# A gated linear attention and its feed-forward on one Trainium2 core: one recorded list of named steps, extended from the first tokens to the second group of feed-forward

## The chip, the core and the metric

The kernel runs on one core of a Trainium2 chip. The core has five engines that run their own queues of instructions in order: PE (matrix multiply), DVE (vector), ACT (scalar functions), POOL (GpSimd) and SP, which here only issues DMAs. The metric is device time in microseconds of one launch, from runs without a profiler. Three runs of the kernel before took 487.58 to 489.64 us, with a median of 488.57 us.

## The reference, cut to what matters

```python
for t in range(S):                                    # B=4, H=8, S=768, D=40
    m_new = maximum(f[t] + m, i[t])                   # running maximum of the gates
    C = exp(f[t] + m - m_new) * C + exp(i[t] - m_new) * outer(v[t], k[t])
    n = exp(f[t] + m - m_new) * n + exp(i[t] - m_new) * k[t]
    y[t] = sigmoid(o[t]) * (C @ q[t]) / maximum(abs(n @ q[t]), 1)
x = y as (B*S = 3072 tokens, H*D = 320)
h = x @ w_in                                          # 320 -> 2048
out = (maximum(h, 0) + alpha * minimum(h, 0)) @ w_out # 2048 -> 320
```

The weights `w_in`, `w_out` arrive as 64-bit floats, the rest as 32-bit ones. Results must have nearly full 32-bit accuracy.

## The kernel before, in words

**Tiles.** The sequence is cut into chunks of 128 tokens: six for each of the four batch rows, 24 in all. Within a chunk the recurrence is written as a masked product of scores, decays and values plus a term from the state left by the chunks before. Two chunks make a group of 256 tokens for the feed-forward, so there are 12 groups.

**Feed-forward.** A group has eight up steps and eight down steps. One up step (`FeedForward.up`) makes 256 hidden channels with 16 matmuls of 256 columns each, since activations and weights are kept as a high and a low part (`XH`, `XL`, `WH`, `WL`; the last 64 of the 320 input channels are in `X2`, `X2L`, `W2`). ACT then takes the negative part (`L722`), DVE applies alpha (`L726`), ACT rounds to the high part `gh` (`L734`), and the low part `gl` is the difference (`L735`), on DVE for the first two groups and on POOL for all later ones. A down step (`L743`) is 12 matmuls of 320 columns.

**Weights.** A block of 64-bit weights is loaded as pairs of 32-bit words and turned into 32-bit floats: ACT scales the upper word (`Weights.scale`, `L816`), DVE shifts it left by three (`L828`) and joins the top bits of the lower word (`L830`). ACT then makes the high part (`L838`) and DVE the low part (`L842`). There are 8 blocks `wi`, 2 blocks `wr` and 8 blocks `wo`. They are staged in tiles that later hold `w_out` parts (`ROOM`), so a block's load waits until the room is free.

**Order.** The first group (chunks 0 and 1, the gates and part of the weights) follows `ORDER`, a string of short step names, and `pin` keeps each engine to that order. Steps named `warmN` are N matmuls of no use on the identity (`L139`); there are 107 of them. Everything after that is emitted by loops, which interleave the up and down steps of groups 0 and 1 with the attention of chunks 2 to 6 (`Side`, `attention`, `stage_a`, `stage_b`). There the compiler's scheduler sets the order in which each engine takes its instructions, and the weights of a block are turned when the loop comes to it (`convert`). From the third group on `ffn` and `late_chunk` do the same for the rest of the program.

**Masks and decays.** For chunks 0 to 3 the decays of a row are spread over the partitions by matmuls into `pb` (`L1016`, `L495`). ACT takes the exponential (`L1027`, `L501`), and POOL zeroes what lies after the token with an affine select (`L1031`, `L505`). Later chunks read the decays from DRAM (`Lb`).

Three DMA queues are in use, and nearly all loads are issued by SP in program order. One instruction there that waits for a buffer holds back all loads behind it.

Of the kernel before, what the change touches and what calls it, by code (L numbers as in the profile page):

```python
# [17 lines left out]
def kernel(ctx: ExitStack, tc: tile.TileContext, q, k, v, i_gate, f_gate, o_gate, w_in, w_out, alpha, out):  # L18
# [68 lines left out]
    pick = const.tile([3 * BH, BH], BF16, tag="pick", name="pick")  # L87

# [175 lines left out]
    def padded_tiles():  # L264


        for j in range(2):
            K = sb.tile([P, 2, 512], F32, tag="kS", name=f"kf{j}", bufs=2)
            nc.gpsimd.memset(K[64:R, 0], 0.0)
            nc.gpsimd.memset(K[:64, 1], 0.0)  # L270
            kpads.append(K)
# [7 lines left out]

    def stage_a(n):  # L280

        pq = psa(f"pq{n}")
        transposed(pq, qn_t[n % NQ])
        K = padded(n)
        qf = sb.tile([P, 512], F32, tag="qf", name=f"qf{n}")
        nc.scalar.copy(qf[:R], pq[:R])
        yield
        pk = psa(f"pk{n}")
        transposed(pk, kn_t[n % NQ])
        padded_copy(K, pk)  # L290
        chunk[n] = (None, K, qf)
        yield
        after(n)
        yield
# [189 lines left out]
    def stage_b(n):  # L484
# [4 lines left out]
        for par in range(2):  # L489
            E = sb.tile([P, 512], F32, tag="E", name=f"E{n}_{par}", bufs=4)  # L490
            if Lb is None:
                pb = psa(f"pb{n}_{par}")
                for p in range(NPR):
# [3 lines left out]
                        LP[:, n % GC * P : (n % GC + 1) * P], start=True, stop=True,  # L497
                    )
            for p in range(NPR):
# [5 lines left out]
            nc.gpsimd.affine_select(  # L505
                out=E, in_=E, pattern=[[0, NPR], [1, P]], base=0, channel_multiplier=-1,
                compare_op=ALU.is_ge, fill=0.0,
            )
# [106 lines left out]
    def attention(n0):  # L615

        late, x_due = iter(()), []
        for _ in stage_a(n0):
            yield
        for n in range(n0, B * NC):  # L620
# [3 lines left out]
            a = stage_a(n + 1) if n + 1 < NDIR else iter(())  # L624
# [24 lines left out]
            if n + 1 == NDIR:  # L649
                far = first_stacks()  # L650
                order = a, bb, late, a, bb, far, bb, far, a, far, far
# [27 lines left out]
    EARLY = 1  # L679
    S1, S2 = 4, 1  # L680
# [4 lines left out]
    V0, V1 = 0, 2  # L685
    FILL = {3: 4, 4: 14, 5: 4}
    ORDER = """dq0 dq1 dw0 dw2 warm24 dv0 dw1 dw4 do1 dw3 do2 scan lf0a lf0b li0 lf0z L0 bj0 qT0 qc0 kT0 kc0 warm12 sp00
        bTt bTc l3a l3b alT l3c l3d warm6 wt0 ex00 sc00 l3e ms00 warm3 sp01 ewj ex01 ms01 sc01 warm3 eeL wg00 wTt eTt
        wTc eTc lf1a lf1b warm3 w0s wg01 sp10 alC ex10 ms10 warm3 sp11 ex11 qT1 w1s kT1 kc1 w0j0 warm4 li1 wd0 w0j1 w2s
# [106 lines left out]
    class Weights:  # L796
# [51 lines left out]
        def all(self):  # L848
            self.scale()
            self.join()  # L850
            for piece in range(len(self.pieces)):
                self.split(piece)
# [473 lines left out]
```

## Time and profile before

| what | value |
| --- | --- |
| runs without profiler, median of 3 | 488.57 us (487.58 to 489.64) |
| profiled execution, own time | 491.87 us |
| its span, first to last instruction | 489.1 us |
| granted TensorE clock, mean | 0.997 |
| busy PE, PE weight load, DVE, ACT, POOL | 473.7, 459.0, 325.3, 310.5, 305.0 us |
| share of the DMA engines taken by packets | 56.6% of the span |
| moved by DMA | 61.60 MB, 126 GB/s over the span |

The profiled execution's own time is 2.8 us above its span, which is launch and end. A busy time counts a matmul until its modelled end, so back-to-back matmuls overlap, and how much useful work PE did is better counted by the distance from one start to the next. A line such as `L735` names the kernel's source line above. "pS<-qf,kf" names the tile that is written and those that are read, without their buffer numbers. In the view by slices a digit is the busy share of one fortieth of the span, 12.2 us.

### The profile page before, as it was taken

The page shows a single profiled execution, that of the slowest core. Times are in us where ns is not written, and L with a number is a line of the kernel's source. Part 1 is how long each engine was busy: PE and PEld are TensorE (multiplying, and loading weights), DVE is VectorE, ACT ScalarE, POOL GpSimd, SP SyncE. Part 2 cuts the span into 40 slices and gives each one's busy share as a digit, 9 for nine tenths or more (in the row PEclk, how much of TensorE's full clock was granted, in tenths as well). Part 3 has the DMA queues.
Part 4 walks back from the last instruction along what each step waited for, and adds up shares of the span by engine and source line. Part 5 has one row for each costly group of instructions (what it writes and reads, how often), then busy time and mean ns, then how long its engine had stood idle before and what let it go on. Part 6 is the DMA issues. An engine that isn't in the chain of part 4 may idle for free.

```text
span 489.1 us, 11907 instructions
## 1 busy us (share of the span) xinstructions
PE 473.7 (97%) x4509; PEld 459.0 (94%) x4509; DVE 325.3 (66%) x679; ACT 310.5 (63%) x692; POOL 305.0 (62%) x394
## 2 busy tenths in 40 slices
PE   8998889999999999999999999999989999999997
PEld 7887778899999999999989999999989999999996
DVE  7889899955676477576495584675694685774321
ACT  3769498645677567676596594776685685553332
POOL 6642063505559859967679779959489598243342
PEclk9999998999999999999999999999999999999999
DMA  9999977354595455687955376677746233000000
GB/s 176 233 167 245 247 196 209 97 107 97 136 205 114 112 138 101 146 188 125 181 146 128 66 188 96 146 168 161 138 127 130 45 99 93 28 1 2 27 1 27
DMA packets 173922, 61.60 MB, mean 126 GB/s; under 512 B 140154, under 2 KB 166122, under 8 KB 173866
## 3 DMA queue, kind: packets, MB, share of 16 engines
q1 hardware_dynamic: 173786, 60.75, 56.6%
q8 instruction: 35, 0.57, 0.5%
q14 instruction: 21, 0.17, 0.1%
q10 hardware_dynamic: 80, 0.11, 0.1%
HBM read 36.90 MB, written 4.03 MB: 84 GB/s over the span
## 4 chain that ended last, share of the span: by engine, by line
PE 66%; DVE 9%; DMA 8%; POOL 6%; issue 4%; ACT 4%; SPq 1%; ACTq 0%; DVEq 0%; POOLq 0%
PE po L743 26%; PE ph L713 4%; PE ph L720 4%; PE ph L717 3%; PE ph L719 3%; PE ph L716 3%; PE ph L714 3%; PE ph L715 3%; PE ph L718 3%; DMA wo<-in_moe_w_out_dram 3%; PE pH L349 3%; DMA qS<-Z 3%; PE pS L445 2%; PE warm L139 2%; POOL gl L735 2%
## 5 line engine op out<-in xcount | busy, mean ns | idle before, releaser
L735 POOL TENSOR_TENSOR gl<-g,gh 128x512 fp32r<-128x512 f32 x80 | 103.0, 1289 | 61.8 <-ACT gh L734 49.3
L726 DVE SCALAR_TENSOR_TENSOR g<-g,oma,ph 128x256 f32<-128x256 f32 x160 | 69.6, 476 | 87.4 <-ACT g L722 82.7
L743 PE MATMUL po<-OH,gh 128*128 128x320 f32 x368 | 109.9, 311 | 0.8 <-ACT gh L734 0.6
L743 PE MATMUL po<-OL,gh 128*128 128x320 f32 x368 | 109.7, 311 | 0.0
L722 ACT ACTIVATE g<-ph 128x512 f32<-128x512 f32 x96 | 57.1, 596 | 44.1 <-PE ph L720 36.2
L734 ACT CAST gh<-g 128x512 fp32r<-128x512 f32 x80 | 49.6, 620 | 41.1 <-DVE g L726 39.8
L743 PEld LDWEIGHTS po<-OH,gh 128*128 128x128 f32 x368 | 69.2, 188 | 1.4 <-ACT gh L734 1.4
L743 PE MATMUL po<-OH,gl 128*128 128x320 f32 x368 | 70.3, 312 | 0.0
L743 PEld LDWEIGHTS po<-OL,gh 128*128 128x128 f32 x368 | 68.9, 188 | 0.0
L713 PE MATMUL ph<-XH,WH 128*128 128x256 f32 x192 | 55.3, 288 | 2.1 <-DVE g L726 1.3
L743 PEld LDWEIGHTS po<-OH,gl 128*128 128x128 f32 x368 | 56.7, 188 | 0.2
L720 PE MATMUL ph<-X2L,W 128*128 128x256 f32 x192 | 54.4, 284 | 0.0
L717 PE MATMUL ph<-X,W 128*128 128x256 f32 x192 | 54.1, 283 | 0.0
L716 PE MATMUL ph<-XH,WL 128*128 128x256 f32 x192 | 54.1, 282 | 0.0
L719 PE MATMUL ph<-XL,WH 128*128 128x256 f32 x192 | 54.1, 282 | 0.0
L714 PE MATMUL ph<-XH,WH 128*128 128x256 f32 x192 | 53.9, 281 | 0.0
L715 PE MATMUL ph<-XH,WL 128*128 128x256 f32 x192 | 53.9, 281 | 0.0
L718 PE MATMUL ph<-XL,WH 128*128 128x256 f32 x192 | 53.7, 280 | 0.0
L336 ACT CAST E<-pS 128x512 bf16<-128x512 f32 x72 | 41.5, 585 | 9.9 <-DVE pS L334 7.3
L420 ACT ACTIVATE E<-Lb,bT 128x128 f32<-128x128 f32 x136 | 42.2, 390 | 2.1 <-PE pH L349 2.0
L713 PEld LDWEIGHTS ph<-XH,WH 128*128 128x128 f32 x192 | 36.4, 190 | 3.2 <-DVE gl L735 1.1
L717 PEld LDWEIGHTS ph<-X,W 128*128 128x128 f32 x192 | 36.2, 189 | 0.0
(202 smaller groups left out, 1134.2 us busy)
## 6 DMA issues: line engine op xcount, KB each, us to landing
Lb<-L_d SPq DMA_DIRECT2D x20, 512.0 KB
wo<-in_moe_w_out_dram SPq DMA_DIRECT2D x8, 640.0 KB
wi<-in_moe_w_in_dram SPq DMA_DIRECT2D x8, 512.0 KB
qn<-in_q_dram SPq DMA_DIRECT2D x24, 160.0 KB
kn<-in_k_dram SPq DMA_DIRECT2D x24, 160.0 KB
va<-in_v_dram SPq DMA_DIRECT2D x24, 160.0 KB
og<-in_o_gate_dram SPq DMA_DIRECT2D x24, 160.0 KB
out_dram<-ob SPq DMA_DIRECT2D x11, 320.0 KB
```

The source lines that it names most:

```text
L713: nc.tensor.matmul(dst, WH[half][:, 0, hs], XH[:, 0], start=True, stop=False)
L714: nc.tensor.matmul(dst, WH[half][:, 1, hs], XH[:, 1], start=False, stop=False)
L715: nc.tensor.matmul(dst, WL[half][:, 0, hs], XH[:, 0], start=False, stop=False)
L716: nc.tensor.matmul(dst, WL[half][:, 1, hs], XH[:, 1], start=False, stop=False)
L717: nc.tensor.matmul(dst, W2[:, fs], X2, start=False, stop=False)
L718: nc.tensor.matmul(dst, WH[half][:, 0, hs], XL[:, 0], start=False, stop=False)
L719: nc.tensor.matmul(dst, WH[half][:, 1, hs], XL[:, 1], start=False, stop=False)
L720: nc.tensor.matmul(dst, W2[:, fs], X2L, start=False, stop=True)
L722: nc.scalar.activation(gt, ph, AF.Relu, scale=-1.0)
L726: nc.vector.scalar_tensor_tensor(out=y[:, e], in0=gt[:, e], scalar=oma[:, f : f + 1], in1=ph[:, e], op0=ALU.mult, op1=ALU.add)
L735: (nc.vector if g < 2 else nc.gpsimd).tensor_tensor(gl, y, gh.bitcast(F32), ALU.subtract)
L743: nc.tensor.matmul(po[j], x[:, e, j * P : (j + 1) * P], W[f // NB][:, f % NB], **ends)
```

## The change

The list `ORDER` is extended so that it names all work through the second group's fourth up and down steps. The tail behind its first `|`, where steps of the later attention (`A`) are interleaved with the rest of group 1, is recorded too but its engine order is the scheduler's. Chunks 2 to 5 are treated as chunks 0 and 1 were (`chunk_steps`, `spread_later`; `stage_a` is gone), so each of their steps has a name and a place. The weights' turning is cut into named steps for each block: `s` (scale, ACT), `y` (shift, DVE) and `j` (join, DVE); or `s`, `x` and `j`, where ACT makes the three low bits (`three`) and one DVE instruction shifts and joins. Then come `h` (high part, ACT) and `l` (low part on DVE) or `p` (low part on POOL). The up steps come in two kinds: U R S G K with the low part on DVE as before, and V r s g N with it on POOL and the result kept in its own tile instead of PSUM.

The masks of chunks 0 to 3 are now added to the decays by one more matmul of 512 columns (`barred`, with a tile `later` that holds a very negative number after the token), and their affine selects on POOL are gone. The three-part decays of chunk 1 (`exact_decays`) are replaced by a plain float32 spread. The scan of the gates is split in two. Of the 107 warming matmuls 18 remain, all at the start; the 22 filling matmuls ahead of the values of chunks 3, 4 and 5 (`FILL`) stay.

In the rows below the numbers of lines are each kernel's own: what stood at `L713` to `L720`, `L726`, `L735`, `L842` and `L828` stands at `L715` to `L722`, `L730`, `L741`, `L860` and `L840` in the changed kernel, whose single shift-and-join is `L846` and whose join alone is `L848`. The numbers behind a tile's name tell its instances apart.

The first place is PE's queue where the first up step (`ph_0`) of group 0 begins. `p` are the transposes of the group's tokens, `pS` scores, `pb` decays spread over partitions, `ps` gates turned to columns. Before:

```order
L545 MATMUL p_0_473<-ident,xn_440 128x128 x2
L545 MATMUL p_0_474<-ident,xn_440 128x128
L139 LDWEIGHTS ident
L139 MATMUL warm<-ident 128x256
...
L982 MATMUL ps_gb_538<-ident,g_WH_94 128x32 x4
L713 MATMUL ph_0_581<-XH_487,WH_100 128x256
```

And now:

```order
L1155 MATMUL pg<-g_gd,unit 104x192
L1064 MATMUL pS_0_439<-qf_398,kf_131 128x128 x4
L1064 MATMUL pS_1_462<-qf_398,kf_131 128x128 x4
L93 LDWEIGHTS ident
L93 MATMUL pb_0_470<-later,ident 128x512
...
L1031 MATMUL pb_0_470<-LP,pick 128x128
...
L715 MATMUL ph_0_502<-XH_444,WH_101 128x256
```

The warming matmuls are gone, and scores and decays of chunk 2 (and, above the piece shown, all transposes of its q and k and the gates' columns of the later chunks) stand ahead of the first up step.

The second place is DVE's queue at the third and fourth up steps of group 0 (`ph_2`, `ph_3`). `t_wi`, `t_wo` are weights being turned, `E` scores times decays, `C` the state, `T` attention results. Before:

```order
L828 TENSOR_SCALAR t_wo_893<-t_wo_893 128x640
L188 TENSOR_TENSOR C_87<-C_86,gamB 40x4x42 x2
L830 SCALAR_TENSOR_TENSOR t_wo_893<-wo_445,t_wo_893 128x640
L735 TENSOR_TENSOR gl_1_890<-ph_1_868,gh_1_889 128x512
L189 TENSOR_TENSOR C_87<-C_87,pu_622 40x4x42
L523 TENSOR_TENSOR E_0_646<-pS_0_657,E_0_646 128x512
```

And now:

```order
L730 SCALAR_TENSOR_TENSOR ph_2_609<-g_2_656,oma,ph_2_609 128x256 x2
L1068 TENSOR_TENSOR E_0_574<-pS_0_660,E_0_574 128x512
L840 TENSOR_SCALAR t_wi_1_671<-t_wi_1_671 128x512
L370 TENSOR_TENSOR T_692<-pI_687,eT 128x336
L848 SCALAR_TENSOR_TENSOR t_wi_1_671<-wi_1_549,t_wi_1_671 128x512
L370 TENSOR_TENSOR T_721<-pI_716,eT 128x336
L730 SCALAR_TENSOR_TENSOR g_3_707<-g_3_707,oma,ph_3_628 128x256 x2
L1201 TENSOR_TENSOR T_721<-T_721,pH_737 128x336
L1068 TENSOR_TENSOR E_1_681<-pS_1_711,E_1_681 128x512
L846 SCALAR_TENSOR_TENSOR t_wo_751<-t_wo_751,wo_733 128x640
```

The low part `gl` of the second up step is on POOL now, and chunks 2 and 3 go through DVE together. The second product of scores and decays of chunk 3 (`E_1_681`) stands ninth in this piece, and the values of chunk 3 wait for it.

The third place is SP's queue of loads after the first weights. `wi`, `wr`, `wo` are weight blocks, `qn`, `kn`, `va`, `og` the chunks' inputs. Before:

```order
L122 DMA og_183<-in_o_gate_dram 128x8x40 x4
L106 DMA va_80<-in_v_dram 128x8x40 x2
L93 DMA qn_76<-in_q_dram 128x8x40
...
L1179 DMA L_d<-g_L 32x768
L806 DMA wi_0_432<-in_moe_w_in_dram 128x1024
L806 DMA wi_1_434<-in_moe_w_in_dram 128x1024
L806 DMA wr_436<-in_moe_w_in_dram 64x1024 x2
L882 DMA wo_445<-in_moe_w_out_dram 128x2x640
```

And now:

```order
L1229 DMA L_d<-g_L 32x768
L814 DMA wi_0_389<-in_moe_w_in_dram 128x1024
L814 DMA wi_1_430<-in_moe_w_in_dram 128x1024
L814 DMA wi_0_452<-in_moe_w_in_dram 128x1024
L897 DMA wo_529<-in_moe_w_out_dram 128x2x640
L814 DMA wi_1_549<-in_moe_w_in_dram 128x1024
L99 DMA qn_76<-in_q_dram 128x8x40
L99 DMA kn_78<-in_k_dram 128x8x40
L112 DMA va_80<-in_v_dram 128x8x40 x2
```

Weight blocks now come as a run of five, and the inputs of chunk 3 follow behind them.

```diff
+    def barred(pb):
+        one = ident.bitcast(BF16).rearrange("p (c w) -> p c w", w=2)[:, :, 1]
+        nc.tensor.matmul(pb, one, later.unsqueeze(1).broadcast_to([P, NPR, P]), start=True, stop=False)
...
-    ORDER = """dq0 dq1 dw0 dw2 warm24 dv0 dw1 dw4 do1 dw3 do2 scan lf0a lf0b li0 lf0z L0 bj0 qT0 qc0 kT0 kc0 warm12 sp00
...
+    ORDER = """warm18 Cz kfz sca0 lf0a lf0z alT dq0 qT0 qc0 sca1 kT0 lf0b L0 sp00 kc0 r0d r0s sc00 li0 i01d bj0 bTt bTc sc01 wt0 r0y
...
+        S06 D03 xa5 D04 R07 S07 o7h xa4 xd4 xd5 o6l D05 G06 G07 K06 K07 o7l D06 D07 Z0 | A A V14 r14 s14 g14 N14 A V15
+        r15 s15 g15 N15 A V16 r16 s16 g16 N16 D14 A V17 r17 s17 g17 N17 D15 A A D16 A D17 A Z1 A"""
...
-            y = ph if g < 2 else gt
+            y = ph if split else gt
...
-            (nc.vector if g < 2 else nc.gpsimd).tensor_tensor(gl, y, gh.bitcast(F32), ALU.subtract)
+            (nc.vector if split else nc.gpsimd).tensor_tensor(gl, y, gh.bitcast(F32), ALU.subtract)
...
-        def join(self, steps=range(2)):
+        def three(self):
+            if self.double:
+                lo = self.raw[..., 0]
+                nc.scalar.activation(lo, lo, AF.Copy, scale=2.0**-29 * (1 - DL), bias=7.5 * DL - 0.5)
+                self.small = True
+
+        def shift(self):
+            if self.double:
+                t = self.t.bitcast(U32)
+                nc.vector.tensor_scalar(t, t, 3, None, ALU.logical_shift_left)
+
+        def join(self):
             if self.double:
                 t, lo = self.t.bitcast(U32), self.raw[..., 0]
...
+                if self.small:
+                    nc.vector.scalar_tensor_tensor(t, t, 3, lo, ALU.logical_shift_left, ALU.bitwise_or)
+                else:
+                    nc.vector.scalar_tensor_tensor(t, lo, 29, t, ALU.logical_shift_right, ALU.bitwise_or)
...
-        def low(self, piece=0):
+        def low(self, piece=0, engine=None):
             t, h, l = self.parts(piece)
-            nc.vector.tensor_tensor(l, t, h.bitcast(F32), ALU.subtract)
+            (engine or nc.vector).tensor_tensor(l, t, h.bitcast(F32), ALU.subtract)
...
+        def spread_later(n, par):
+
+            pb = psa(f"pb{n}_{par}")
+            barred(pb)
...
         def decay(n, par):
+            if n >= 2 * GC:
+                E[n, par] = decays_of(n, par, pre[n])
+                yield
+                return
...
-            nc.gpsimd.affine_select(
-                out=e, in_=e, pattern=[[0, NPR], [1, P]], base=0, channel_multiplier=-1,
-                compare_op=ALU.is_ge, fill=0.0,
-            )
...
-        def exact_decays():
...
+        def chunk_steps(n):
+
+            steps[f"wd{n}"] = lambda: weighed(n)
+            steps[f"v{n}"] = lambda: values_of(n)
...
+        def named_ffn(g):
...
+                for tokens, split in (("URSGK", True), ("VrsgN", False)):
+                    add(" ".join(f"{x}{g}{fp}" for x in tokens), lazily(lambda split=split: ffs[g].up_steps(split)))
+                steps[f"D{g}{fp}"] = lambda fp=fp: ffs[g].down(fp)
...
+            self.it, self.pos = attention(NDIR), 1 + 6 * (NDIR - GC)
...
-    f0, f1 = FeedForward(0), None
-    for fp in range(NP + BEHIND + 1):
...
+    queue(start, len(nc.cur_bb.bb.instructions), pinned)
     while 2 not in x_tiles:
         side.step()
```

More of the change, by code (lines that the diff above doesn't have):

```diff
@@ L1181, in first_group @@
         )
-        add("l3a l3b l3c l3d l3e", exact_decays())
         add("lpa lpb lpc lpd lpe", later_decays())
@@ new lines, in first_group @@
+        for g in range(2):
+            named_ffn(g)
+        add("tp0 tp1 tp2 tp3", lazily(first_stacks))
+        add("um6 uc6", lazily(lambda: update_steps(NDIR)))
+        steps["wd6"] = lambda: weighed(NDIR)
+        add("vp0 vp1", lazily(lambda: value_parts(NDIR)))
+        pieces = ORDER.split("|")
+        for piece in pieces:
+            for name in piece.split():
+                if name.startswith("warm"):
+                    warm(int(name[4:]))
+                elif name == "A":
+                    side.step()
+                else:
+                    steps[name]()
+            yield
```

377 lines of the change are left out of this document (175 added, 202 removed).

## Prediction

> **What bounds the kernel now.** I read the page by slices first, then busy times by stretch, then what PE does in the first stretches.
>
> ```profile
> PE   8998889999999999999999999999989999999997
> PEclk9999998999999999999999999999999999999999
> DMA  9999977354595455687955376677746233000000
> ```
>
> ```profile
> core 0: us, PE busy (x) PEld busy (x) DVE busy (x) ACT busy (x) POOL busy (x), PEclk, DMA share, GB/s
> 0.00:32.35 32.35, 29.68 (x251) 25.31 (x251) 26.45 (x51) 16.34 (x40) 20.01 (x40) 1.00 1.07 193
> 32.35:60.00 27.65, 24.33 (x236) 22.29 (x234) 24.36 (x56) 19.75 (x41) 4.11 (x6) 1.00 0.91 244
> 60.00:80.00 20.00, 17.33 (x143) 15.15 (x141) 18.51 (x34) 18.74 (x48) 9.97 (x12) 0.91 0.76 213
> 80.00:100.00 20.00, 19.30 (x161) 18.36 (x160) 19.23 (x37) 13.35 (x29) 8.82 (x10) 1.00 0.43 110
> 100.00:134.70 34.70, 34.50 (x271) 33.79 (x270) 20.45 (x37) 19.21 (x37) 13.10 (x20) 1.00 0.53 113
> 134.70:489.00 354.30, 348.59 (x3459) 344.07 (x3457) 216.26 (x470) 223.10 (x501) 248.94 (x307) 1.00 0.50 108
> ```
>
> From 100 us on PE is full and sets the time. The change can only win in the first 100 us, where PE is not full, DVE is (88 of 100 us) and POOL is nearly empty between 32 and 60 us (4.11 of 27.65). Part of the "busy" PE there is useless besides:
>
> ```profile
> L139 PE MATMUL warm<-ident 128*128 128x256 bf16 x107 | 16.3, 299 | 1.4 <-POOL ident masks.py:199 1.4
> L139 PE MATMUL pH<-ident 128*128 128x256 bf16 x22 | 4.4, 362 | 0.5 <-DVE E L523 0.5
> 32.35 0.39 PE L713 MATMUL ph<-XH,WH 128*128 128x256 f32 x1
> 401.71 0.28 PE L713 MATMUL ph<-XH,WH 128*128 128x256 f32 x1
> 402.66 0.31 PE L743 MATMUL po<-OH,gh 128*128 128x320 f32 x1
> 403.83 0.28 PE L713 MATMUL ph<-XH,WH 128*128 128x256 f32 x1
> ```
>
> Useful work I count from start to start. Eight up matmuls take 0.95 us (401.71 to 402.66), so an up step takes 1.9 us; eight down matmuls take 1.17 us (to 403.83), so a down step takes 1.76 us. The first up step starts at 32.35 us. By PE's queue only 9.4 us of useful work stand ahead of it, about 84 float32 matmuls at a similar distance of 0.11 us. About 23 us of that stretch are filler and waiting. The third group's first up step starts after 134.7 us. Ahead of it stand 16 up and 15 down steps (30.4 + 26.4 us) and attention and transposes worth some 41 us, together 98 us. So between the first up step and 134.7 us (102.35 us) PE does 88.6 us of work and loses 13.7, of which the rows show 6.9 as idle (27.65, 20.00, 20.00, 34.70 less their busy times) and 4.4 as filler. The rest is matmuls that trickle.
>
> **The change, part by part. Work moved.** These are the prices:
>
> ```profile
> L842 DVE TENSOR_TENSOR WL<-t_wi,WH 128x512 fp32r<-128x512 f32 x8 | 5.7, 718 | 0.4 <-ACT WH L838 0.4
> L735 DVE TENSOR_TENSOR gl<-ph,gh 128x512 fp32r<-128x512 f32 x12 | 8.2, 687 | 5.1 <-ACT gh L734 5.0
> L735 POOL TENSOR_TENSOR gl<-g,gh 128x512 fp32r<-128x512 f32 x80 | 103.0, 1289 | 61.8 <-ACT gh L734 49.3 <-issue 11.7 <-POOL gl L735 0.8
> L828 DVE TENSOR_SCALAR t_wo<-t_wo 128x640 uint32<-128x640 uint32 x8 | 5.1, 633 | 1.9 <-ACT t_wo L816 1.8
> L816 ACT ACTIVATE t_wi<-wi 128x512 f32<-128x512 f32 x8 | 5.2, 673 | 0.3 <-DVE W L842 0.3
> ```
>
> DVE gives up 13 of 20 weights' low parts (13 x 0.72 = 9.4 us), 10 of 16 `gl` (6.9), 9 of 18 shifts (0.55 each, the row's 633 ns holding some waits: 5.0) and the five exact-decay steps (1.7): 23 us, of which new small pieces take 1. POOL takes 23 subtractions at 1.29 us (29.7) and drops eight selects (0.9 each, by a row below: 7): +23. ACT takes nine more activations like `L816` (+6). Up to 134.7 us the first five rows above sum to DVE 109, ACT 87 and POOL 56 us, so they become about 87, 93 and 79, beside PE's 99.7 (98 and eight masks of 512 columns, 0.21 us each, twice a filler's 0.11). All four would fit into 110 us, and little reserve is left on any.
>
> **The start.** DVE works without a gap from 16 us to the second half's tokens:
>
> ```profile
> 16.00 3.02 DVE L147 TENSOR_TENSOR kd<-kn,wT 128x320 f32<-128x320 f32 x1
> 30.05 0.49 DVE L407 TENSOR_TENSOR xn<-T,og 128x320 f32<-128x320 f32 x1
> 30.60 0.75 POOL L411 COPY xn<-xn 128x64 f32<-128x64 f32 x1 [1.87 <-DVE xn L407]
> 11.14 0.90 POOL L1031 TENSOR_SCALAR_AFFINE_SELECT E<-E 128x512 f32<-128x512 f32 x1 [1.67 <-ACT E L1027]
> 12.08 0.69 DVE L1051 TENSOR_TENSOR E<-pS,E 128x512 f32<-128x512 f32 x1 [0.53 <-POOL E L1031]
> ```
>
> The durations of DVE's instructions up to that `xn` sum to 26.3 us in the queue before and to 22.6 in the new one, 3.6 less, and the select's 0.9 us between exponential and product is gone. So `xn` can end at 26.9 instead of 30.5. POOL then stands in the way: after the copy come two subtractions, a last piece of the decays (0.66) and a `kd` (0.8), so the first up step starts near 30 rather than at 28.5. Ahead of it now stand 13.9 us of work, 1.3 of them masks. Time not worked falls from 22.9 to 17.4 us (16.1 and the masks): **5.5 us gained**.
>
> **The middle.** From 30 us I followed the new queues with the same durations. PE runs four up steps nearly closed up to 40 us, then waits where DVE's queue is full: about 2 us for chunk 3's values behind `E_1_681`, 1 us at the fifth up step, 1.5 us before chunk 4's values, 1 us for chunk 6's scores, which wait for the transposes by DMA. With the 22 fillers (2.4 to 4.4 us) that makes 9, and I add 2 for small waits that such a walk misses. Against 13.7 lost before: **2.7 us gained** (bounds: -1, if nothing closes and trickle grows; 9, if DVE's 22 us all turn into time). I take the low third, since four engines at 80 to 100% in fixed order leave no slack. The last two masks' pair costs **0.4**.
>
> **The clock.** What the 89 removed matmuls did besides nothing is seen where PE starves:
>
> ```profile
> 16.78 1.91 PE L139 MATMUL warm<-ident 128*128 128x256 bf16 x16
> 72.84 0.44 PE L545 MATMUL p<-ident,xn 128*128 128x128 f32 x2 [1.11 <-POOL xn L407]
> 73.78 3.14 PE L139 MATMUL pH<-ident 128*128 128x256 bf16 x14 [0.51 <-DVE E L523]
> 72.00:74.00 2.00, 0.66 (x4) 0.42 (x5) 2.00 (x4) 1.94 (x4) 2.00 (x4) 0.93 0.56 57
> 74.00:76.00 2.00, 2.00 (x11) 1.40 (x10) 1.94 (x3) 1.95 (x4) 1.07 (x1) 0.50 1.01 370
> 76.00:78.00 2.00, 2.00 (x16) 1.80 (x15) 1.97 (x4) 0.89 (x3) 0.00 (x0) 0.71 1.14 340
> ```
>
> After a stretch with little work (four matmuls in 2 us) the granted clock is one half for some 3.4 us, and 14 fillers take 3.14 us where 16 took 1.91 at 16.78 us. In the new start PE has 12 us of work between 5 and 30 us. I count two such stretches of thin work (near 13 and near 24 us) and one in the middle, of which half lies beside other waits: **2 us lost** (bounds 0 and 13, below). "TensorE: Matmul & The Clock Gate" of the Trainium skill, under "What's actually happening", has the clock fall only after a whole idle window of about 3.4 us. By that rule nothing is lost here and the sum improves by 2 us; the trace disagrees, since the stretch ahead of 74 us was not idle.
>
> **The loads.** The DMA engines were close to full for the first 60 us:
>
> ```profile
> DMA packets 31462, 13.00 MB, mean 217 GB/s; under 512 B 27120, under 2 KB 29184, under 8 KB 31456
> 36.17 5.74 DMA wo<-in_moe_w_out_dram
> 50.76 9.16 DMA wo<-in_moe_w_out_dram
> ```
>
> The packets are those of the first 60 us, in which the first fence's DMA row shows tenths of 7 and 9, and the chain of waits has ACT waiting 5.74 and 9.16 us for blocks of `w_out`. SP's new order puts 12.6 MB up to the seventh `wi` block, which at 217 GB/s has landed at 59 us; ACT comes to it near 57. Each late block holds all behind it on ACT: **1 us lost** (bounds 0 and 5).
>
> The sum is 5.5 + 2.7 - 0.4 - 2 - 1 = 4.8 us, off a profiled execution of 491.87 us: 487.1. The median of the runs lies 3.3 us lower at 488.57, so there I expect 483.8, rounded to 484.0.
>
> **The rivals.** *The clock stays halved* (slower). The warming matmuls may be what carries PE through its thin stretches. The 16.1 us not worked by 30 us and the middle's waits hold up to nine stretches of 3.4 us with work below the amount seen ahead of 74 us; each adds its own work once more, some 1.5 us, 13 in all. Without the clock's term the sum is 6.8, so from five such stretches on the gain is gone, and with all nine the time is 494.8. For it speaks that one such stretch lost the clock; against it that the stretch from 57.65 to 60 us, with five matmuls or so and an idle time of 1.57 us, did not (the clock's mean up to 60 us is 1.00):
>
> ```profile
> 57.65 0.60 PE L226 MATMUL pk<-ident,kn 128*104 128x128 f32 x4
> 59.82 0.38 PE L495 MATMUL pb<-LP,pick 96*128 96x128 bf16 x4 [1.57 <-ACT qf L286]
> ```
>
> *DVE stays full* (no change). DVE's work from SBUF may wait while POOL reads:
>
> ```profile
> 15.29 0.79 DVE L828 TENSOR_SCALAR t_wi<-t_wi 128x512 uint32<-128x512 uint32 x1
> 21.60 0.42 DVE L828 TENSOR_SCALAR t_wi<-t_wi 128x512 uint32<-128x512 uint32 x1
> 15.87 1.16 POOL L1097 TENSOR_TENSOR g_lf<-g_lf,g_WL 32x512 f32<-32x512 f32 x1
> ```
>
> The same shift took 0.79 us next to POOL's instruction and 0.42 alone, and `kd`, begun at 16.00 while that one ran, took 3.02 us. If each of the 26 joins, shifts and low parts left on DVE meets one of POOL's 23 new subtractions and waits half of it (0.65 us), 16.9 of DVE's 22 us are gone, the middle gains nothing and the start 2 us less: 3.5 - 0.4 - 2 - 1 = 0.1 us, 488.5. Against it speaks the mean of `L842`, two inputs from SBUF, 718 ns: little above the 687 of `L735` on DVE, which reads one of its two from PSUM. "SBUF — State Buffer", section "Who interferes with whom", of the Trainium skill calls this an exclusive lock, by which it is each collision and not the mean that counts; the trace agrees in the two rows of `L828`.
>
> *It packs.* The planner's list closes the middle's waits to 4 us with fillers and the clock holds: 5.5 + 9 - 0.4 = 14 gained, 474.5. For it: all four sums are under 100 us. Against it: fixed queues on four nearly full engines.
>
> **How the numbers follow.** Forecast (480 to 486.2) 0.46, packs (474 to 480) 0.18, DVE full (486.2 to 491) 0.19, clock (491 to 496) 0.17. About 0.5%, 2.4 us, is what a measurement tells from no change. So faster 0.64, same 0.19, slower 0.17. The range runs from 475 to 491, leaving out the best of the third rival and most of the first; the forecast's own is 480 to 486.2.
>
> **What would show it.** The start is right if the first up step begins near 30 us with PE's scores of chunk 2 behind it; the middle, if DVE's busy time up to the third group falls by about 20 us and POOL's rises as much, and the third group begins near 130 us. The clock's row would show one half in two or three places before 60 us. After that the two traces should run alike. The forecast is wrong if the first up step comes later than 32 us, if the clock is half for more than 15 us in all, or if PE waits in that stage for DMA.

## The result, and the profile after

| | before | changed |
| --- | --- | --- |
| median of 20 runs each, us | 489.99 (487.58 to 492.75) | 488.21 (482.97 to 494.99) |
| ratio | | 0.9941 (0.9916 to 0.9967) |
| profiled execution, own time, us | 491.87 | 490.43 |
| its span, us | 489.1 | 488.7 |

The change is 0.6% faster where 0.9% was forecast (1.8 us between the medians, where 4.6 were forecast). The ratio leaves out the runs that lie more than 1.5% above the fastest of their kernel, among them the changed kernel's profiled one, which is why the ratio is a little better than that of the medians. The median lies in the predicted range, but in part by luck. It is above the forecast's own 480 to 486.2 us, in the band that was given to *DVE stays full*, and DVE did not stay full. In the profiled execution three parts were off by 5 to 6 us each, two losses and one gain that was larger than forecast and hid one of them.

The first sign is the scatter. The kernel before ran within 5 us, the changed one within 12. The slices of the changed kernel's profile show two places where the granted clock was lower, one in the start and one near 170 us:

```profile
PE   8999999999999799999989999999899999999996
PEclk9959999999999989999999999999999999999999
DMA  9977988968974656579445367588672431000000
```

Its span and mean granted clock (0.997 in the kernel before):

```profile
core 0: 488.7 us, clock 0.983
```

The same stretches as before, by engine (in each row busy time and number of instructions of PE, its weight loads, DVE, ACT and POOL, then clock, DMA share and GB/s; the third group begins earlier, so the last two are cut at 128.2 us):

```profile
0.00:32.35 32.35, 30.18 (x201) 25.17 (x202) 21.02 (x49) 20.52 (x48) 21.04 (x41) 0.85 0.92 200
32.35:60.00 27.65, 27.25 (x267) 25.63 (x267) 20.04 (x40) 21.71 (x48) 10.60 (x10) 0.93 0.80 172
60.00:80.00 20.00, 18.28 (x163) 17.35 (x162) 18.57 (x39) 17.64 (x41) 14.30 (x16) 1.00 0.84 199
80.00:100.00 20.00, 19.72 (x159) 19.42 (x158) 13.91 (x25) 15.67 (x30) 15.50 (x20) 1.00 0.92 213
100.00:128.20 28.20, 28.07 (x253) 27.25 (x252) 19.73 (x39) 23.07 (x57) 18.05 (x23) 1.00 0.81 171
128.20:488.70 360.50, 348.42 (x3407) 342.79 (x3405) 209.94 (x460) 218.45 (x487) 248.03 (x304) 1.00 0.48 103
```

The work moved as the diff says. DVE is busy for 303.2 us in all, where it was 325.3, POOL 327.5 after 305.0, ACT 317.1 after 310.5. DVE is no longer full between 80 and 100 us (13.9 of 20, before 19.2).

Three instants cut each execution into start, middle and late part: the first up step and the gate of the third group's first up step, from the timeline, and the last gate, from the view of the gates' line (first and last start stand behind the durations). The kernel before, whose first up step at 32.35 us is quoted above:

```profile
136.86 0.60 ACT L722 ACTIVATE g<-ph 128x512 f32<-128x512 f32 x1
```

```profile
L722 ACT ACTIVATE g<-ph x96: 570/598/617, 36.2 to 480.6; 128x512 f32<-128x512 f32 x96
```

The changed kernel:

```profile
35.67 0.52 PE L715 MATMUL ph<-XH,WH 128*128 128x256 f32 x1
130.38 0.60 ACT L725 ACTIVATE g<-ph 128x512 f32<-128x512 f32 x1
```

```profile
L725 ACT ACTIVATE g<-ph x96: 577/598/659, 38.8 to 479.7; 128x512 f32<-128x512 f32 x96
```

| part of the profiled execution, us | before | changed | change | forecast |
| --- | --- | --- | --- | --- |
| start, to the first up step | 32.35 | 35.67 | +3.3 | -2.4 (near 30), and part of the clock's +2 |
| middle, from there to the third group's first gate | 104.5 | 94.7 | -9.8 | -3.1 (work done ahead of it), -2.7, masks +0.4, loads +1 |
| late, from there to the last gate | 343.7 | 349.3 | +5.6 | 0 |
| behind the last gate | 8.5 | 9.0 | +0.5 | 0 |

The 5.5 us that the prediction calls the start's are 2.4 in the time of the first up step and 3.1 of work that is already done by then, which shortens the middle. The middle gained 9.8 us for 4.4 forecast. The start lost, and from the third group on most of the rest went. The experiments had to find out why.

**The start.** In stretches of 3.41 us, columns as in the view above, with the two places where the clock fell:

```profile
18.96:22.37 3.41, 3.41 (x31) 3.36 (x30) 3.30 (x10) 3.41 (x8) 1.27 (x3) 1.00 0.69 181
22.37:25.78 3.41, 3.41 (x18) 3.40 (x18) 3.31 (x6) 1.86 (x4) 1.66 (x2) 0.50 0.96 290
32.61:36.02 3.41, 3.41 (x19) 2.80 (x19) 0.10 (x1) 1.99 (x6) 1.99 (x2) 0.50 0.88 146
169.14:172.56 3.42, 1.53 (x13) 1.56 (x14) 3.42 (x8) 2.78 (x7) 3.42 (x6) 1.00 1.09 294
172.56:175.97 3.41, 3.41 (x27) 3.21 (x26) 1.77 (x4) 1.61 (x4) 3.41 (x4) 0.50 0.31 54
```

The clock is half from 22.37 to 36.02 us, exactly four such stretches, and again from 172.56 to 175.97. The second place is what one expects, a stretch with PE half idle ahead of it. The first is not: ahead of 22.37 us PE was busy without a gap. What it did there, with the rows just before and a later one, from the timeline:

```profile
17.44 0.51 PE L175 MATMUL pu<-va,kd 128*40 128x42 f32 x16
19.14 1.98 PE L305 MATMUL pH<-va,E 128*128 128x42 f32 x16
20.95 1.10 PE L359 MATMUL pI<-C,qf 104*128 104x84 f32 x8
21.89 3.11 PE L305 MATMUL pH<-va,E 128*128 128x42 f32 x16
30.43 3.78 PE L1064 MATMUL pS<-qf,kf 104*128 104x128 f32 x16
```

Mostly matmuls of 42 and 84 columns with float32 weights. Those of `pH` follow each other at 0.112 us, the same distance as those of 128 columns (`pS`), while 16 with 42 columns and weights 40 wide (`pu`) take 0.51 us in all. So it is not the columns that set the 0.112 us. That it is the load of the wide weights fits these rows, but was not measured apart. While the clock is half, 16 rows of score matmuls take 3.78 us and not 1.8.

The chain of work that ended last shows what the half clock cost here. In the changed kernel it runs through PE alone from 7.75 us to behind the first up step (four of its pieces):

```profile
7.75 1.15 PE pb L1019 x8
16.43 1.09 PE pS L1064 x8
22.05 2.94 PE pH L305 x16
30.50 3.71 PE pS L1064 x16
```

Three profiles have this same start, that of the change, of the change again and of the shift alone (both below). Their clock was half for 13.65, 37.55 and 10.24 us ahead of the first up step, which began at 35.67 us (above), 47.19 and 33.91:

```profile
47.19 0.36 PE L715 MATMUL ph<-XH,WH 128*128 128x256 f32 x1
33.91 0.36 PE L715 MATMUL ph<-XH,WH 128*128 128x256 f32 x1
```

The line through the three is 29.0 us plus 0.48 us for each microsecond at half clock. By this estimate the first up step would begin at 29 us without the loss, and the loss cost 6.7 us of the start in the profiled execution.

Over the 20 runs of the changed kernel the span follows the clock: with the time at half clock taken as twice (1 - mean clock) times the span, the line through the 20 points is 481.1 us plus 0.38 us for each microsecond at half clock. The best two runs have 481.3 us at a clock of 0.996 and 0.994, the worst 493.3 us at 0.968, the middle of the clocks is 0.986 (13.7 us at half clock, 5.2 us of time).

**The late part.** PE's wait ahead of the up steps' first matmul, from 130 to 400 us, before and now (count, busy, mean, idle before):

```profile
L713 PE MATMUL ph<-XH,WH 128*128 128x256 f32 x120 | 34.5, 287 | 1.3 <-DVE g L726 1.3
```

```profile
L715 PE MATMUL ph<-XH,WH 128*128 128x256 f32 x118 | 33.9, 287 | 6.5 <-DVE g L730 6.5
```

The largest of these waits ends at 171.03 us, and is the one behind which the clock falls. From the timelines of PE, DVE and POOL:

```profile
171.03 0.35 PE L715 MATMUL ph<-XH,WH 128*128 128x256 f32 x1 [2.33 <-DVE g L730]
169.02 0.49 DVE L399 TENSOR_TENSOR xn<-pI,og 128x320 f32<-128x320 f32 x1 [2.07 <-POOL og L397]
170.02 0.86 DVE L730 SCALAR_TENSOR_TENSOR g<-g,oma,ph 128x256 f32<-128x256 f32 x2
166.16 0.81 POOL L246 TENSOR_TENSOR qr<-qn,Z 128x320 f32<-128x320 f32 x1
168.25 0.73 POOL L397 TENSOR_TENSOR og<-og,r 128x320 f32<-128x320 f32 x1
```

DVE stood 2.07 us at a chunk's tokens (`xn`), which waited for POOL, and the alpha step of an up step was queued behind it.

### The profile page after: what moved, and what is told of

Read it like the earlier page. It is cut to its first block, busy times and chain, and to the rows that moved or that the text cites. A ratio compares the mean times of both kernels' runs of the same rounds, so it can differ in the third digit from the quotient of the medians.

```text
span 488.7 us, 11761 instructions
## 1 busy us (share of the span) xinstructions
PE 471.9 (97%) x4436; PEld 457.6 (94%) x4436; DVE 303.2 (62%) x647; ACT 317.1 (65%) x706; POOL 327.5 (67%) x410
## 4 chain that ended last, share of the span: by engine, by line
PE 70%; DMA 9%; DVE 6%; ACT 6%; POOL 5%; issue 3%; SPq 0%; ACTq 0%; DVEq 0%; POOLq 0%
PE po L750 27%; PE ph L715 4%; PE ph L717 3%; PE ph L716 3%; PE ph L721 3%; PE ph L718 3%; PE ph L720 3%; PE ph L719 3%; PE ph L722 3%; PE pS L1064 2%; DMA qS<-Z 2%; DMA kS<-Z 2%; PE pH L341 2%; DMA wr<-in_moe_w_in_dram 2%; PE pS L437 2%
## 5 line engine op out<-in xcount | busy, mean ns | idle before, releaser
L741 POOL TENSOR_TENSOR gl<-g,gh 128x512 fp32r<-128x512 f32 x89 | 115.0, 1296 | 75.9 <-ACT gh L739 71.6
L730 DVE SCALAR_TENSOR_TENSOR g<-g,oma,ph 128x256 f32<-128x256 f32 x180 | 78.2, 475 | 94.5 <-ACT g L725 88.8
L750 PE MATMUL po<-OH,gh 128*128 128x320 f32 x368 | 111.9, 315 | 0.5 <-ACT gh L739 0.4
L739 ACT CAST gh<-g 128x512 fp32r<-128x512 f32 x89 | 55.1, 620 | 39.3 <-DVE g L730 38.8
L715 PE MATMUL ph<-XH,WH 128*128 128x256 f32 x192 | 55.6, 290 | 7.0 <-DVE g L730 6.5
L412 ACT ACTIVATE E<-Lb,bT 128x128 f32<-128x128 f32 x152 | 47.3, 390 | 16.3 <-PE pH L341 14.1
L720 PE MATMUL ph<-XL,WH 128*128 128x256 f32 x192 | 54.4, 283 | 0.0
L722 PE MATMUL ph<-X2L,W 128*128 128x256 f32 x192 | 53.6, 279 | 0.0
L328 ACT CAST E<-pS 128x512 bf16<-128x512 f32 x72 | 41.4, 586 | 7.2 <-DVE pS L326 5.8
L715 PEld LDWEIGHTS ph<-XH,WH 128*128 128x128 f32 x192 | 36.2, 188 | 8.7 <-ACT E L328 6.6
```

The lines of the kernel that those rows point to most:

```text
L715: nc.tensor.matmul(dst, WH[half][:, 0, hs], XH[:, 0], start=True, stop=False)
L720: nc.tensor.matmul(dst, WH[half][:, 0, hs], XL[:, 0], start=False, stop=False)
L722: nc.tensor.matmul(dst, W2[:, fs], X2L, start=False, stop=True)
L730: nc.vector.scalar_tensor_tensor(out=y[:, e], in0=gt[:, e], scalar=oma[:, f : f + 1], in1=ph[:, e], op0=ALU.mult, op1=ALU.add)
L741: (nc.vector if split else nc.gpsimd).tensor_tensor(gl, y, gh.bitcast(F32), ALU.subtract)
L750: nc.tensor.matmul(po[j], x[:, e, j * P : (j + 1) * P], W[f // NB][:, f % NB], **ends)
```

## Experiments

All are compared with the kernel before in the same batch. "Wide matmul" is the kernel's own warming matmul on the identity, 256 columns in 0.107 us.

### Wide and narrow matmuls where the clock fell

```diff
-  ... lpb v0 gr0 ...   fm1 gg0 v1 ...
+  ... lpb v0 warm4 gr0 ...   fm1 warm4 gg0 v1 ...
```

> Eight matmuls of 256 columns on the identity (0.107 us each, 0.86 us in all) are put back into the changed kernel, four before and four after the scores-times-state matmuls of chunk 1, where the clock fell at 22.37 us in its profile; on every other engine the order is the same as in the change. Theory (clock): the clock is decided in windows of 3.41 us by how long matmuls stream columns; between 19 and 25 us the change streams for only 0.39 of a window, since 42 columns take 35 ns and the float32 weights 112 ns. With the eight it streams for 0.6, the clock does not fall there, the first up step starts near 31 us and not at 35.7, the median is 484 to 485.5 us, and highest less lowest is under 7 us where the change has 12. Rival (given back later): the lead at the third group is lost again at later hand-overs whatever the clock does in the start; the median stays at 488, within 1 us.

```diff
-  ... lpb v0 gr0 ...   fm1 gg0 v1 ...
+  ... lpb v0 thin4 gr0 ...   fm1 thin4 gg0 v1 ...
+        def thin(n=1):
+            for _ in range(n):
+                nc.tensor.matmul(junk[:, :32], ident, ident[:, :32], start=True, stop=True)
```

> At the same two places eight float32 matmuls of 32 columns: by the rows of the gates' matmuls each takes the same 0.107 us of PE's time, but streams for only 27 ns. Theory (clock by streamed columns): they do not hold the clock (a window near 20 us streams for 0.4 or less), so the median is that of the change, 488 to 489 us, and so is the scatter. Rival (clock by PE being occupied): they do what the wide ones do, 484 to 485.5 us. Rival (given back later): no difference between the two kernels.

| | median | lowest to highest | median clock | ratio to before |
| --- | --- | --- | --- | --- |
| wide | 485.94 | 485.71 to 498.69 | 0.992 | 0.9905 (0.9866 to 0.9943) |
| narrow | 491.65 | 487.75 to 503.04 | 0.978 | 0.9993 (0.9964 to 1.0022) |

The clock decides: the wide ones raise it and the time falls, the narrow ones do not, and by the ratios they are some 2.5 us slower than the change. (A narrow one appears as two rows of 0.11 us, so the eight cost 0.9 us more than expected. That is a sixth of the 5.7 us between the two.) But the expectation for the wide ones held for five runs of seven only. Two had a clock of 0.964 and took 498.7 us, the profiled one among them. There the clock fell at 14.1 us, and in the stretch ahead of it PE was busy with matmuls of mostly 128 columns and more (two rows of its timeline, then the two stretches around the fall):

```profile
11.38 1.15 PE L1019 MATMUL pb<-g_L,ident 32*128 32x128 f32 x8
12.88 1.15 PE L1019 MATMUL pb<-g_L,ident 32*128 32x128 f32 x8
```

```profile
10.69:14.10 3.41, 3.41 (x26) 2.70 (x26) 2.09 (x4) 2.54 (x11) 2.49 (x2) 1.00 1.17 246
14.10:17.50 3.40, 3.40 (x15) 2.73 (x15) 2.52 (x5) 3.19 (x8) 1.12 (x1) 0.50 1.17 149
```

So columns alone are not it: by the count given in the last section they fill 0.78 of that stretch. The 16 matmul rows shown read 32 of 128 rows. If each matmul counts its streaming time times the share of the rows that it reads, that stretch has 0.37 of a window, and the one ahead of 22.37 us in the change 0.35.

### The kernel before without its warming

```diff
-    ORDER = """dq0 dq1 dw0 dw2 warm24 dv0 ... kc0 warm12 sp00 ... l3d warm6 wt0 ...
+    ORDER = """dq0 dq1 dw0 dw2 warm18 dv0 ... kc0 sp00 ... l3d wt0 ...
```

> The kernel before with 18 warming matmuls at its start and none of the other 83. Theory (clock): the streamed share of its windows between 5 and 32 us, 0.5 to 0.9 with the warming, falls by up to 0.5 per window, so the clock is half for 10 us or more; the first up step starts 1 to 4 us later than 32.35, and the median is 2 to 5 us above the kernel before. Rival (the warming matmuls only sit in waits and the start is bound by DVE): within 1 us of the kernel before, also where the clock falls.

Of the 107 matmuls 26 are left in its profile and 81 are out, since eight more than expected stay among the values of chunk 1. It took 507.33 us (505.19 to 509.78), ratio 1.0335 (1.029 to 1.038), at a clock of 0.952 to 0.963. That is 16 us lost, more than three times the most expected. The view by stretches of its profile:

```profile
8.60:42.80 34.20, 32.42 (x164) 29.75 (x163) 21.30 (x49) 18.21 (x44) 13.25 (x15) 0.50 0.85 174
100.80:107.60 6.80, 5.64 (x22) 5.65 (x23) 3.72 (x10) 1.69 (x5) 1.69 (x3) 0.50 0.49 115
```

Its first up step starts at 37.7 us and the third group at 148.7. The removed matmuls were not filler in the sense of the prediction: in the kernel before they were worth 16 us.

### The shared work put back on DVE

```diff
-  ... i00p ... r0p r0H i10x ... r0P ... o4p ... o3p ...
+  ... i00l ... r0l r0H i10y ... r0L ... o4l ... o3l ...
```

Twelve low parts of weights go from POOL to DVE (`p`, `P` to `l`, `L`), nine shifts from ACT to DVE (`x` to `y`).

> The changed kernel with 12 low parts of weights put back from POOL to DVE and the nine shifts put back from ACT to DVE; PE's order and everything else stays. DVE gets about 12 x 0.72 + 9 x 0.55 = 13.6 us back in the first 85 us, POOL loses 15.5 and ACT 6. Theory (sharing frees DVE): half of this comes back as waits of PE before 85 us, so the third group begins 4 to 7 us later than the change and the median is 2 to 5 us above it. Rival (DVE stays full through the port that it shares with POOL): within 1 us of the change. The clock adds up to 5 us of scatter to either.

493.15 us (490.3 to 503.97), ratio 1.0048 (1.0016 to 1.008), at a median clock of 0.984, about the change's. So the sharing is worth 1.1%, or 5 us, a little above the upper end expected. The profiled execution shows where: first up step and third group's first gate:

```profile
41.95 0.37 PE L715 MATMUL ph<-XH,WH 128*128 128x256 f32 x1
142.16 0.60 ACT L725 ACTIVATE g<-ph 128x512 f32<-128x512 f32 x1
```

The middle takes 100.2 us against the change's 94.7. Of these 5.5 us up to 1.7 can be the clock, which in this profile was half from 72.07 to 75.48 us too, so the sharing is worth some 4 to 5.5 there. The late first up step is the clock again, which was half from 14.0 to 41.4 us. The rival that DVE stays full through a shared port falls.

### Holding the clock through the start, and the later attention

```diff
-  ... alT dq0 qT0 qc0 sca1 kT0 lf0b ... sc00 li0 ...   r0j sp01 ewj ...
+  ... alT dq0 qT0 warm4 qc0 sca1 kT0 warm4 lf0b ... sc00 warm3 li0 ...   r0j sp01 warm3 ewj ...
```

> The eight wide matmuls of the first experiment and 14 more like them between 5 and 13 us: four behind each of the first two transposes, three behind chunk 0's scores, three behind its last decays' spread. 2.4 us of PE's time in all, of which about 0.7 lie in waits. Theory (clock): counted as time in which columns stream, weighted by the rows in use, the first experiment's profile has 0.37 of the window at 10.7 us and loses the clock there, and the change 0.35 of the window at 19 us; all falls of six profiles have 0.39 or less, and a fall lasts until a window with 0.83. With the 14 no window before 25 us is under 0.45, so in no run the clock's mean is under 0.985; median 1 to 4 us below the change on this chip, no run more than 6 us above the fastest. Rival (given back later): median within 1 us of the change.

> The change once more, unaltered, on the chip of the other three: the reference for them. 0.4 to 0.8% below the kernel before, with runs over 10 us apart and a mean clock between 0.965 and 0.996.

```diff
-    OFF = 0
+    OFF = -2
```

> The kernel with all 22 wide matmuls, in which the later attention's steps are asked for two thirteenths of a group (some 5 us) later against the feed-forward from the third group on. In the change's profile the group's last tokens are ready 20 us ahead of the gate that needs them (186.0 against 206.2), in the kernel before 8 (200.7 against 208.4), and DVE waits at tokens whose queries came late by DMA (166.2 and 168.3 us on POOL) with the gates behind it. Theory (given back later, attention too early): the waits of 0.9 to 2.3 us at 168, 208, 244 and 282 us shrink; median 2 to 4 us below the kernel with 22 wide matmuls alone. Rival (the scheduler's order is as good either way): within 1 us of it.

```diff
-    OFF = 0
+    OFF = -4
```

> The same with four thirteenths (some 11 us) later, which gives the lead that the kernel before had. Theory (attention too early): 3 to 5 us below the kernel with 22 wide matmuls. Rival: within 1 us of it; or slower, if now the tokens come too late for their up steps.

| | median | lowest to highest | median clock | ratio to before |
| --- | --- | --- | --- | --- |
| the change again | 487.89 | 485.43 to 501.51 | 0.987 | 0.9918 (0.989 to 0.9946) |
| 22 wide | 485.37 | 483.75 to 497.91 | 0.993 | 0.988 (0.9836 to 0.9925) |
| 22 wide, two thirteenths later | 483.37 | 482.01 to 484.31 | 0.999 | 0.9848 (0.9809 to 0.9886) |
| 22 wide, four thirteenths later | 483.29 | 482.47 to 494.33 | 0.996 | 0.9853 (0.9815 to 0.9891) |

The change repeats, with one of its runs at 501.5 us and a clock of 0.959. Four of six runs with the 22 hold the clock; two still lost it (0.966 and 0.962), so "in no run" was wrong: counted in its profile, windows of 3.41 us with 0.33 and 0.31 remain, from 12.0 and 26.5 us on. With the later attention asked for later, the medians are 2 us lower, and in both profiles no wait near 165 us takes the clock down. Much of the 2 us is the runs that lost the clock: without them the medians are 484.05, 483.37 and 482.81 us, so of the 2 to 4 and 3 to 5 us expected only about 1 is left, and the intervals of the ratios overlap. Two or four thirteenths make no difference.

To part the two losses, the shift alone, without any added matmul, and then all of it with 11 more wide matmuls at the places where the profile still came near the fall:

```diff
-    OFF = 0
+    OFF = -2
```

> The changed kernel, without any added matmul, with the later attention two thirteenths of a group later. Theory (two separate losses): the clock is lost in the start as in the change (mean 0.965 to 0.99), but not near 170 us, and the later waits shrink: median 1 to 3 us below the change, 485 to 487 us. Rival (the later gain needs the held start): as the change, 488 us within 1.

```diff
-  ... r0j sp01 warm3 ewj ...   qT2 kT2 i00h ...   wlc x0 x1 ...
+  ... r0j sp01 warm6 ewj ...   qT2 kT2 warm4 i00h ...   wlc warm4 x0 x1 ...
```

> The kernel with 22 wide matmuls and the later attention two thirteenths of a group later, with 11 more wide matmuls where its profile still comes near the fall: three more behind chunk 0's last decays (0.34 of a window that begins at 12.5 us), four behind the first transposes of chunk 2 and four ahead of the tokens' transposes (0.32 at 27.0 us). 1.2 us of PE's time, of which 0.4 lie in a wait. Theory (clock by streamed columns times rows): the mean clock is 0.99 or more in every run and highest less lowest under 4 us; the median is 482 to 484.5 us, the same as without the 11 within 1 us, since only a rare loss is left to avoid. Rival: losses of 10 us and more still occur in one run of six, so something beside this sum sets the clock.

The shift alone gives 487.19 us (483.51 to 499.63), ratio 0.991 (0.9871 to 0.9949), clock 0.986: not to be told from the change (0.9918). Its profile has a late part of 350.0 us, no better than the change's 349.3, although the waits ahead of the up steps from 130 to 400 us are 2.8 us there and not 6.5: the clock fell at 234.35 us instead. So the shift is not shown to shorten the late part by itself.

All of it gives 483.72 us (480.7 to 486.29), ratio 0.9853 (0.9804 to 0.9903). No run has a clock below 0.996 and none is far out, as with the 22 and two thirteenths, in six runs each. The spread is 5.6 us where under 4 was expected, with 486.29 us at a clock of 1.0, so some scatter has another cause. Its profiled execution, in the views used above: span and clock, the third group's first gate, all gates, and PE's wait ahead of the up steps from 130 to 400 us:

```profile
core 0: 479.0 us, clock 1.000
```

```profile
125.67 0.60 ACT L725 ACTIVATE g<-ph 128x512 f32<-128x512 f32 x1
```

```profile
L725 ACT ACTIVATE g<-ph x96: 573/597/663, 36.3 to 470.1; 128x512 f32<-128x512 f32 x96
```

```profile
L715 PE MATMUL ph<-XH,WH 128*128 128x256 f32 x119 | 34.1, 287 | 1.9 <-DVE g L730 1.9
```

The late part is 344.4 us, that of the kernel before within 1. Over the eleven profiles with the new list it is 348.2 to 351.5 us in the seven whose clock fell somewhere behind 160 us, and 344.4 to 345.9 in the four without such a fall. One of these four is the next version, which has neither the shift nor a held start. So neither is needed for a short late part, and neither is shown to cause it. This version and the one with 22 wide matmuls and the shift beat both kernels, the one before by 1.5% and the change by some 4 us.

### The same matmuls with a quarter of the rows

```diff
+        def quarter(n=1):
+            x = ident.bitcast(BF16)
+            for _ in range(n):
+                nc.tensor.matmul(junk[:, : 2 * P], x[:32, :P], x[:32], start=True, stop=True)
```

It stands in the list where the 22 wide ones stood.

> The kernel with 22 wide matmuls, but each of the 22 reads only 32 of the 128 rows: the same 256 columns streamed, the same 0.107 us. Theory (columns times rows): they count a quarter, so the start loses the clock about as the change does, with a median of the clock's mean near 0.985 (0.993 with all rows), and the median time is 488 to 490 us. Rival (columns alone): as with all rows, 485.4 us within 1, clock 0.993.

497.84 us (490.21 to 506.23), ratio 1.0127 (1.0063 to 1.019), at a median clock of 0.963. The same number of the same columns at the same places, with 32 rows instead of 128, does not hold the clock, and is 12 us slower than with all rows. Rows count. It is worse than expected, 10 us slower than the change itself. The 22 matmuls' own 2.4 us are the smaller part of that; the clock is lower too (0.963 after 0.987 in the change again), which is 9 us by the line through the 20 runs. Why 22 matmuls of few rows lose more of the clock than none was not tested.

## Why the prediction was wrong, step by step

**The start, +5.5 us: near in time, on the wrong path.** The first up step came at 35.67 us, not near 30. By the line through three profiles it would come at 29.0 without the clock's loss, and with the clock at 1.0 and 33 wide matmuls (3.5 us) in the start it comes at 32.3 us in the filled version's profile, so the 30 itself was about right. That is partly luck. The prediction built it from the queues of DVE and POOL and gave PE 13.9 us of work ahead of it, counting each float32 matmul once at 0.11 us. Most of them are two rows in the trace, 0.11 us apart: the eight scores of a chunk are the `x16` above. Without the warming 200 rows stand ahead of the first up step, by their distances an estimate of 20 us, where the kernel before has 144 and some 14 us, not 9.4. So PE was no longer the engine that waits.

**The clock, -2 us: the step that failed.** It was the right mechanism at the wrong size and with the wrong cause. The prediction looked for stretches in which PE waits, found two near 13 and 24 us and one in the middle, gave them one window of 3.4 us each, and let half of that lie beside other waits. What counts is not only whether PE waits. A start made of narrow or few-rowed matmuls is thin for the clock although PE never stops, once the clock is half it stays so through 13.65 us (in another execution 37.5), and with PE on the chain there is little to hide it behind. The middle run's 13.7 us at half clock cost 5.2 us by the line through the 20 runs, 3.2 more than the term, and the worst run lost 12. So the first rival (*the clock stays halved*) had the mechanism, but its band (491 to 496 us) holds two of the 20 runs; four lie in the forecast's and 14 between the two. Two signs that the prediction gave for being wrong came with it: a first up step later than 32 us, and a clock at half for more than 15 us in all (17.1 in the profile). "TensorE: Matmul & The Clock Gate" of the Trainium skill, under "What's actually happening", has the fall come after a whole idle window. The trace disagrees: the window ahead of 22.37 us has 3.41 of 3.41 us busy.

**The middle, +2.7 us: mis-sized.** Of the 9.8 us measured 3.1 were to come from work done ahead of the first up step. Against the 1.3 us that the other terms come to stand some 6.7, within the upper bound of 9 that was given for the first of them. I took the low third "since four engines at 80 to 100% in fixed order leave no slack". The fixed order did pack: from 32.35 to 60 us PE is busy for 27.25 us with 267 rows, where it was 24.33 with 236. The sharing alone is worth some 4 to 5.5 us of it, and up to 1.7 more is the window at half clock that the kernel before lost at 73.74 us and the changed one did not. So the rival *it packs* was nearer about this stage.

**DVE stays full: wrong.** The collisions are there. By the groups up to the third group, the joins that are left on DVE take longer than before (first the kernel before, then the changed one; behind the first bar stand busy us and mean ns):

```profile
L830 DVE SCALAR_TENSOR_TENSOR t_wo<-wo,t_wo 128x640 uint32<-128x640 uint32 x8 | 7.1, 892 | 0.1
L830 DVE SCALAR_TENSOR_TENSOR t_wi<-wi,t_wi 128x512 uint32<-128x512 uint32 x8 | 6.4, 798 | 0.1
```

```profile
L848 DVE SCALAR_TENSOR_TENSOR t_wi<-wi,t_wi 128x512 uint32<-128x512 uint32 x4 | 4.6, 1154 | 0.0
L848 DVE SCALAR_TENSOR_TENSOR t_wo<-wo,t_wo 128x640 uint32<-128x640 uint32 x4 | 4.3, 1065 | 0.1
```

That is 0.36 and 0.17 us each, 2 us over the eight, and the eight shifts left beside them take some 1.4 us more than such shifts did before. DVE gave up 22 us. In the version with the shared work back on DVE the same joins take 0.78 and 0.94 us, so the longer ones go with POOL's new subtractions.

**The loads, -1 us: came at another block.** ACT's waits for blocks of `w_out` fell:

```profile
L816 ACT ACTIVATE t_wo<-wo 128x640 f32<-128x640 f32 x8 | 6.3, 804 | 5.6 <-DMA wo<-in_moe_w_out_dram 5.6
```

```profile
L824 ACT ACTIVATE t_wo<-wo 128x640 f32<-128x640 f32 x8 | 6.3, 791 | 1.0 <-DMA wo<-in_moe_w_out_dram 1.0
```

But ACT now waits for a `wr` block, and the chain that ended last has 10.29 us of that block's load, from 45.55 us on:

```profile
55.95 0.67 ACT L824 ACTIVATE t_wr<-wr 128x512 f32<-128x512 f32 x1 [2.27 <-DMA wr<-in_moe_w_in_dram]
```

What this cost in time was not measured apart, nor were the masks' 0.4 us.

**"After that the two traces should run alike": wrong, 5.6 us.** This is the other term that failed, and it was not even in the sum. No line of the later stages is edited, but the order of their instructions is the scheduler's, and here it comes out otherwise: counted back from the end, the names in the two profiles agree for the last 235 of PE's some 3,400 matmul rows behind the third group's first gate, and for the last 22 of DVE's some 470. The new order has 5.2 us more of waits ahead of up steps, and one of them costs a window at half clock besides. In the filled version the late part is as short as before with an earlier head, so the loss is not owed to the head's being earlier as such. What exactly in the order makes it stays open.

## What to carry to other kernels

A warming matmul that lies beside a thin stretch is worth what the clock is worth there, not its own 0.1 us, so before any is taken out, count for each window of 3.41 us what PE does, by columns and rows, and not whether it is busy. Time an edit that takes them out in many runs, since the windows lie differently in each launch. And where a scheduler orders what follows, compare the order of the untouched part too before its time is put at zero.

## What the runs showed of the hardware

The granted clock changes on a grid of 3.41 us (22.37 and 172.56 us in one profile are 44 steps apart), and the grid lies differently in each execution. In all 13 profiles together, without the last 15 us of each, where PE runs out of work and the clock falls too, a simple count tells the changes. Each matmul record of the trace counts 0.42 ns per column (256 columns in 0.107 us), float32 ones of fewer than 256 columns twice that (128 in 0.112 us), times the rows that it reads over 128, and while the clock is half all of this counts double, as the matmuls take twice as long. All 18 falls follow a window with 0.13 to 0.39 of this; of 1,682 windows behind which the clock stayed full, only four have less than the highest of these 18, and the lowest has 0.37. All 18 returns follow a window with 0.77 or more; of 50 windows behind which it stayed half, two have more than the lowest of these, and the highest has 0.78. The weights of this count were chosen to fit these profiles; that columns alone do not do was shown by the matmuls with 32 rows (without the rows two falls follow a window with 0.77, and over 200 windows that kept the clock have less), and that PE's being busy does not by the narrow ones. So in these profiles a window with less than 0.37 of work always lost the clock and one with more than 0.39 never did, while it took 0.77 or more to return it.
